# Moving work across the edges of the stages: weight gradients that start inside the GLU stage, an FFT chain paced ahead of them, and constants that are made first

## The chip, the cores and the metric

The kernel runs on one core of a Trainium2 chip. The metric is the device time of one execution in microseconds (us). The kernel before takes 695.69 us, the median of three runs (695.45 to 695.86). Engines are called PE (TensorE, the matrix engine), DVE (VectorE), ACT (ScalarE), POOL (GpSimd) and SP (SyncE, here a queue of DMA issues). Every engine works through its own instructions in program order.

## The reference

The kernel computes the output and all nine gradients of a gated block over 2048 tokens of width 512, in bfloat16. The forward function is:

```python
xn = layernorm(x)
# A: short convolution over 4 tokens, product with v, long convolution by FFT
k_shift = sum(k_pad[:, t:t + S] * shift_k[:, ks - 1 - t] for t in range(4))
kv = k_shift * v
y = irfft(rfft(kv_pad) * rfft(ssm_k_pad))[:S] + kv * ssm_D
s = xn * y
# B: gated linear unit, F = 1376
h = sigmoid(xn @ w_gate) * (xn @ w_up)
g = silu(h @ w_down)
out = x + s * g
```

`reference` returns `out` (out_0) and the gradients of `grad_out` with respect to q (out_1), k (out_2), v (out_3), shift_k (out_4), ssm_k (out_5), ssm_D (out_6), w_gate, w_up and w_down (out_7 to out_9).

## The kernel before

Tokens are cut into 16 tiles of 128, channels into four groups (cg) of 128, and F into 11 blocks of 128. The program has three stages.

**Stage A** (0 to 173 us) runs four generators side by side. `strK` and `strV` make the FFT's inputs from ssm_k and from the short convolution (`acc`, `term`, `kvt` on DVE), `strX` multiplies in the frequency domain and transforms back (tiles ps_q, ps_fl, ps_x, ps_b, ps_y), and `strG` runs the GLU's forward part (`f_gen`, tile psGU) for the first LAG = 3 token tiles. `gen_fft_consts` makes the FFT's matrices Cf, BD and R. The buffer `Bg` holds the last inverse step's input; ps_y reads it.

**The GLU stage** (173 to some 440 us) is `stepB`. For tile i it takes, in turn, `d_gen` (ps_dzT, psD), `f_gen` of tile i + 3 (ps_xnT, psGU), `z_gen` of tile i + 1 (psZ) and `x_gen` (psX). `z_gen` reads w_down in `wd`; `d_gen` reads its transpose `wdT`. Three arrays of results, h, dg and du, are turned by DMA transposes and stored to hS_d, dgS_d and duS_d in DRAM.

**The FFT backward stage** (to 660 us, and a drain) is `frontC` (ps_q) and `backC` (flips ps_fl, then ps_x, a complex product on DVE, ps_b, ps_y, ps_dk and ps_diag) for the four channel groups. Beside it `dW` makes the three weight gradients: 9 jobs, three sources times three column chunks (512, 512, 352), 35 blocks of 16 matmuls in all, tile psW. `ld_L(n)` loads the source of job n in four pieces, into one of two buffers in `Lbufs`.

Three things set the order. `run_streams` takes a list of generators with a budget, a start and an end: the one whose (start + (end − start) x work done / budget) is lowest goes next, so the numbers pace one generator against another. Tile's scheduler then reorders instructions within their dependencies. And `Bal.evac` gives each eviction from PSUM to ACT or DVE, whichever has the smaller sum of estimated work, unless the call names an engine. SBUF is one slab; a `Ring` is a piece of it, and freed pieces are handed out again, so a load into a new Ring waits for the last reader of the bytes that it covers.

PSUM: in stage A three two-bank tiles and two for transposes; in the later stages two two-bank tiles ("mm"), two for accumulation ("acc": psZ, psX, psW) and two for transposes.

Lines that the text speaks of (of the kernel before): L322 psGU, L325 the product that frees it, L596 the load of `wd`, L615 psZ, L626 the last product of dz, L660 psD, L679 psX, L749 `ld_L`, L765 and L768 psW, L121 and L124 the eviction on ACT and on DVE.

Of the kernel before, what the change touches and what calls it, by code (L numbers as in the profile page):

```python
# [16 lines left out]
P = 128  # L17
# [135 lines left out]
def gen_fft_consts(nc, ar, negpi, Cf, BD, R):  # L153
# [12 lines left out]
    m = tmp([16, 128], i32)  # L166
    mc = tmp([2, 16, 128], i32)
    for h in range(2):
        js = slice(8 * h, 8 * h + 8)
        nc.vector.tensor_tensor(m[:, js], a[:, js, None].to_broadcast([P, 8, 128]),  # L170
                                b[:, None, :].to_broadcast([P, 8, 128]), ALU.mult)
        nc.vector.tensor_single_scalar(mc[:, 0, js], m[:, js], 6144, ALU.add)
        nc.vector.tensor_single_scalar(mc[:, 0, js], mc[:, 0, js], 8191, ALU.bitwise_and)
        nc.vector.tensor_single_scalar(mc[:, 1, js], m[:, js], 8191, ALU.bitwise_and)
        nc.scalar.activation(Cf[:, :, js], mc[:, :, js], ACT.Sin, bias=negpi, scale=sc)
# [29 lines left out]
    for c, ci, t in ((0, 0, 0), (0, 1, 1), (1, 0, 2), (1, 1, 0)):  # L205
        nc.vector.tensor_scalar(R[:, c, :, :, ci], tri[:, t], SCALE_INV, None, ALU.mult)
    for r in rings:
        r.free()
# [7 lines left out]
def kernel_impl(ctx, tc, A_q, A_k, A_v, A_shift_k, A_ssm_k, A_ssm_D, B_x, B_w_gate, B_w_up, B_w_down,  # L216
# [19 lines left out]
    def ps_mm(shape, dt=f32, name="ps_mm"):  # L236
        return PS["pool"].tile([P] + shape, dt, name=name, tag="mm", bufs=PS["mm"])

    def ps_acc(shape, dt=f32, name="ps_acc"):
        return PS["pool"].tile([P] + shape, dt, name=name, tag="acc", bufs=2)  # L240

    def ps_tr(shape, dt=bf16, name="ps_tr"):
        return PS["pool"].tile([P] + shape, dt, name=name, tag="tr", bufs=2)
# [62 lines left out]
    def f_gen(i):  # L306
# [4 lines left out]
        bal.evac(xnT, pt[:], 512, half=True, eng="v")  # L311
# [5 lines left out]
        for pi, (f0, nb) in enumerate(FBS):  # L317
            ps = ps_mm([2, 4, 128], name="psGU")
            for k, w in ((0, wg), (1, wu)):
                for b in range(nb):  # L320
                    for db in range(4):
                        nc.tensor.matmul(ps[:, k, b, :], w[:, db, (f0 + b) * 128:(f0 + b + 1) * 128], xnT[:, db, :],  # L322
                                         start=(db == 0), stop=(db == 3))
            nc.scalar.activation(sigT[:, f0:f0 + nb, :], ps[:, 0, 0:nb, :], ACT.Sigmoid)  # L324
            nc.vector.tensor_tensor(hT[:, f0:f0 + nb, :], ps[:, 1, 0:nb, :], sigT[:, f0:f0 + nb, :], ALU.mult)  # L325
# [7 lines left out]

    psA = tc.tile_pool(name="psA", bufs=1, space=PSUM)
# [662 lines left out]
```

## Time and profile before

| what | value |
|---|---|
| median of 3 runs | 695.69 us |
| the profiled execution: its time, its span | 698.14 us, 696.4 us |
| PE busy | 558.4 us, 80% of the span |
| DVE busy | 440.2 us, 63% |
| ACT busy | 321.9 us, 46% |
| POOL busy | 143.3 us, 21% |
| moved by DMA | 114.51 MB, 164 GB/s on average |
| mean granted clock of PE | 0.94 |

In the rows that follow, a timeline row reads: start in us, length in us, engine, line, operation, tile written <- tile read, count of instructions, and in brackets the idle time ahead of it with what ended that. The matmuls of one row run one behind the other; the length covers the whole row. A row of windows reads: stretch, its length, busy time and number of instructions of PE, PE's weight loads, DVE, ACT and POOL, then the granted clock as a share, the busy share of DMA, and GB/s. A row of waits reads: who waited for whom, total us, number of times, longest.

### The profile page before, as it was taken

To read this page: it belongs to the slowest core of one execution; us is meant where nothing else is said; L and a number is where in the kernel's file an instruction comes from. 1 tells how busy PE (TensorE), PEld (TensorE's weight loads), DVE (VectorE), ACT (ScalarE), POOL (GpSimd) and SP (SyncE) were. 2 spreads that over 40 slices of the span, in tenths; PEclk is the share of its full clock that TensorE was granted. 3 is DMA by queue.
4 is the path that set the end of the run, shared out by engine and by line. 5 is a ranking of instruction groups with operands and counts; after the bars stand their busy time and mean duration, and the time that the engine had idled before them with its cause. 6 is when DMAs were issued, how large, how long until landed. Compare 5 with 4: busy or idle time off the path is not lost. (4 is left out here: it accounts for less than half of the span.)

```text
span 696.4 us, 12768 instructions
## 1 busy us (share of the span) xinstructions
PE 558.4 (80%) x5184; PEld 377.2 (54%) x5252; DVE 440.2 (63%) x888; ACT 321.9 (46%) x375; POOL 143.3 (21%) x242
## 2 busy tenths in 40 slices
PE   1577875976899999998999788469879999999800
PEld 0465754654666667766776445225455565656500
DVE  5988995645766777776776733203837739459450
ACT  4555693974333343342333213212582774664710
POOL 3022140331011111211111111131221243132020
PEclk9889998998999999999999999879999999999955
DMA  9444246497566666766767878955525479633094
GB/s 285 138 133 166 101 153 121 136 273 184 128 165 178 165 162 189 164 156 173 175 158 184 221 199 191 224 133 182 195 84 163 138 240 341 205 100 109 12 110 41
DMA packets 140962, 114.51 MB, mean 164 GB/s; under 512 B 91190, under 2 KB 126472, under 8 KB 140904
## 3 DMA queue, kind: packets, MB, share of 16 engines
q1 hardware_dynamic: 123224, 52.90, 34.2%
q0 software_dynamic: 16624, 57.98, 27.3%
q10 hardware_dynamic: 1056, 2.82, 1.1%
q8 instruction: 41, 0.67, 0.4%
q14 instruction: 17, 0.14, 0.1%
HBM read 49.18 MB, written 42.51 MB: 132 GB/s over the span
## 5 line engine op out<-in xcount | busy, mean ns | idle before, releaser
L322 PE MATMUL psGU<-slab 128*128 128x128 bf16 x1408 | 90.1, 223 | 9.0 <-DVE slab L325 4.7
L322 PEld LDWEIGHTS <-slab 128*128 128x128 bf16 x1408 | 85.1, 100 | 15.7 <-issue 13.7
L768 PE MATMUL psW<-slab 128*128 128x512 bf16 (+1 forms) x371 | 84.6, 356 | 1.1 <-ACT slab L121 0.5
L679 PE MATMUL psX<-slab 128*128 128x512 bf16 x336 | 79.6, 385 | 6.1 <-DVE slab L666 5.4
L121 ACT CAST slab<-ps_b 128x1024 bf16<-128x1024 f32 x48 | 49.0, 1023 | 37.8 <-PE ps_b L459 37.6
L459 PE MATMUL ps_b<-slab 128*128 128x256 bf16 x384 | 56.1, 279 | 12.0 <-DVE slab L448 10.6
L324 ACT ACTIVATE slab<-psGU 128x512 bf16<-128x512 f32 (+1 forms) x48 | 27.1, 564 | 69.3 <-PE psGU L322 69.2
L121 ACT CAST slab<-ps_x 128x1024 bf16<-128x1024 f32 x48 | 48.4, 1031 | 22.3 <-PE ps_x L439 21.5
L124 DVE COPY slab<-ps_fl 128x1024 bf16<-128x1024 bf16 x48 | 32.1, 687 | 40.3 <-PE ps_fl L428 40.0
L688 ACT ACTIVATE slab<-slab 128x512 f32<-128x512 f32 x16 | 13.1, 816 | 95.4 <-DVE slab L687 95.4
L679 PEld LDWEIGHTS <-slab 128*128 128x128 bf16 x352 | 33.3, 99 | 42.0 <-DVE slab L666 6.8
L121 ACT CAST slab<-ps_q 128x1024 bf16<-128x1024 f32 x48 | 48.6, 1044 | 15.4 <-PE ps_q L418 15.4
L765 PE MATMUL psW<-slab 128*128 128x512 bf16 (+1 forms) x172 | 40.9, 391 | 17.8 <-DMA slab<-hS_d 14.7
L459 PEld LDWEIGHTS <-slab 128*128 128x128 bf16 x384 | 35.5, 99 | 34.4 <-DVE slab L448 21.5
L768 PEld LDWEIGHTS <-slab 128*128 128x128 bf16 x384 | 36.6, 98 | 28.5 <-issue 0.8
L121 ACT CAST slab<-psW 128x512 bf16<-128x512 f32 (+2 forms) x35 | 20.3, 579 | 60.5 <-PE psW L765 40.9
L660 PE MATMUL psD<-slab 128*128 128x128 bf16 x704 | 46.3, 219 | 0.6 <-ACT slab L121 0.6
L660 PEld LDWEIGHTS <-slab 128*128 128x128 bf16 x704 | 41.8, 98 | 4.5 <-issue 0.7
L445 DVE TENSOR_TENSOR slab<-slab 128x1024 bf16<-128x1024 bf16 x48 | 33.1, 690 | 14.5 <-ACT slab L121 9.4
L615 PE MATMUL psZ<-slab 128*128 128x512 bf16 x162 | 39.7, 379 | 1.8 <-ACT slab L121 1.1
L418 PE MATMUL ps_q<-slab 128*128 128x128 bf16 x384 | 31.1, 230 | 11.4 <-DVE slab L518 5.3
L765 PEld LDWEIGHTS <-slab 128*128 128x128 bf16 (+1 forms) x176 | 17.9, 103 | 39.2 <-DMA slab<-hS_d 15.4
(154 smaller groups left out, 1008.1 us busy)
## 6 DMA issues: line engine op xcount, KB each, us to landing
KK_d<-slab POOLq DMA_DIRECT2D x32, 256.0 KB, 2.8
slab<-KK_d POOLq DMA_DIRECT2D x16, 512.0 KB, 4.2
out_dram<-slab POOLq DMA_DIRECT2D x58, 128.0 KB, 3.0
hS_d<-slab POOLq DMA_DIRECT2D x16, 352.0 KB, 2.7
dgS_d<-slab POOLq DMA_DIRECT2D x16, 352.0 KB, 3.8
duS_d<-slab POOLq DMA_DIRECT2D x16, 352.0 KB, 3.1
slab<-in_A_q_dram SPq DMA_DIRECT2D x32, 128.0 KB, 2.3
slab<-hS_d SPq DMA_DIRECT2D x8, 512.0 KB, 6.0
```

The costliest lines, as they stand in the source:

```text
L121: self.nc.scalar.copy(dst, src)
L124: self.nc.vector.tensor_copy(dst, src)
L322: nc.tensor.matmul(ps[:, k, b, :], w[:, db, (f0 + b) * 128:(f0 + b + 1) * 128], xnT[:, db, :], start=(db == 0), stop=(db == 3))
L324: nc.scalar.activation(sigT[:, f0:f0 + nb, :], ps[:, 0, 0:nb, :], ACT.Sigmoid)
L418: nc.tensor.matmul(ps[:, jj, :], Cf[:, c, j, :], src(j), start=True, stop=True)
L445: nc.vector.tensor_tensor(out=T1, in0=K, in1=X[:, 0:1, :].to_broadcast([P, 2, 512]), op=ALU.mult)
L459: nc.tensor.matmul(ps[:, gg].rearrange("p j x -> p (j x)"), Y[:, c, gg * 128:(gg + 1) * 128], R[:, c].rearrange("p j e c -> p (j e c)"), s ...
L615: nc.tensor.matmul(psZ[:], hT[:, fb, :], wd[:, fb, :], start=(fb == 0), stop=(fb == NFB - 1))
L660: nc.tensor.matmul(psD[:, b, :], wdT[:, db, (f0 + b) * 128:(f0 + b + 1) * 128], dzT[:, db, :], start=(db == 0), stop=(db == 3))
L679: nc.tensor.matmul(psX[:], srcT[:, fb, :], wT[:, fb, :], start=(n == 0), stop=(n == 2 * NFB - 1))
L765: nc.tensor.matmul(acc[0:kf, :], L[:, j, b * 128:b * 128 + kf], dzA[:, j, :], start=(j == 0), stop=(j == NJ - 1))
L768: nc.tensor.matmul(acc[:, 0:w], xnA[:, j, b * 128:(b + 1) * 128], L[:, j, 0:w], start=(j == 0), stop=(j == NJ - 1))
```

## The change

The change has five parts.

1. *Start.* `gen_fft_consts` is emitted first, and in it Cf behind BD and R. w_gate and w_up are loaded from SP's queue, behind the first q tile, ssm_k and k, where ACT issued them before; the second q tile and v come behind them. The loads of ssm_D and shift_k go from POOL's queue to ACT's.
2. *Evictions.* Those that named an engine (ps_xnT, ps_ci, ps_fl, ps_kt on DVE; ps_dzT on ACT) are now given by the balance.
3. *PSUM of the GLU stage.* In place of two two-bank tiles there are four of one bank: psG and psU apart, psD in blocks of 4, 4 and 3.
4. *Weight gradients.* The budget of `stepB` is set to the sum of its work (522 000 where it was 286 720), so dW's start at 0.9 lies beside its last tenth. `wd` and the five buffers of `z_gen` are freed when psZ of tile 15 is emitted; the second load buffer goes there, and loads 0 and 1 are both issued. The pieces of slab are laid out anew for that.
5. *FFT stage.* `frontC` is paced to 0.5 (before 0.75), `backC` from −0.05 to 0.72 (before 0.03 to 0.95), beside dW from 0 to 1.

```diff
@@ gen_fft_consts: the Cf part (m, mc, ACT.Sin) moves behind BD and R
...
@@ f_gen
-            ps = ps_mm([2, 4, 128], name="psGU")
-            for k, w in ((0, wg), (1, wu)):
+            if PS["wide"]:
+                ps = ps_mm([2, 4, 128], name="psGU")
+                pg, pu = ps[:, 0], ps[:, 1]
+            else:
+                pg, pu = ps_mm([4, 128], name="psG")[:], ps_mm([4, 128], name="psU")[:]
+            for pt_, w in ((pg, wg), (pu, wu)):
...
@@ stage A, start
     f_x(0)
-    nc.scalar.dma_start(wg[:, :, 0:F], B_w_gate.rearrange("(db p) f -> p db f", p=P))
-    nc.scalar.dma_start(wu[:, :, 0:F], B_w_up.rearrange("(db p) f -> p db f", p=P))
+    ld_KT(0)
+    ld_k(0)
+    nc.sync.dma_start(wg[:, :, 0:F], B_w_gate.rearrange("(db p) f -> p db f", p=P))
+    nc.sync.dma_start(wu[:, :, 0:F], B_w_up.rearrange("(db p) f -> p db f", p=P))
     f_x(1)
-    ld_KT(0)
-    ld_kv(0)
+    ld_v(0)
+    gen_fft_consts(nc, ar, negpi, Cf, BD, R)
...
@@ flip (and likewise ps_xnT, ps_ci, ps_kt; ps_dzT had eng="a")
-                bal.evac(Qf[:, c, gb * 8:(gb + 1) * 8, :], pt[:], 1024, half=True, eng="v")
+                bal.evac(Qf[:, c, gb * 8:(gb + 1) * 8, :], pt[:], 1024, half=True)
...
@@ GLU stage
-    psB = ctx.enter_context(tc.tile_pool(name="psB", bufs=1, space=PSUM, reuse_waits="tile"))
-    PS["pool"], PS["mm"] = psB, 2
+    PS["acc"] = ctx.enter_context(tc.tile_pool(name="psW", bufs=1, space=PSUM, reuse_waits="tile"))
+    psB = tc.tile_pool(name="psB", bufs=1, space=PSUM, reuse_waits="tile")
+    PS["mm"], PS["n"], PS["wide"] = psB.__enter__(), 4, False
...
+    zd_blk = ar.alloc(16384)
+    ar.release(zd_blk)
+    zw = {k: Ring(ar, [D]) for k in ("sigz", "gate", "s_out", "dgate", "t2")}
     wd_r, wdT_r, wgT_r, wuT_r = Ring(ar, [NFB, D]), Ring(ar, [4, FP]), Ring(ar, [NFB, D]), Ring(ar, [NFB, D])
...
@@ d_gen
-        for f0, nb in ((0, 8), (8, 3)):
-            psD = ps_mm([8, 128], name="psD")
+        for f0, nb in FBS:
+            psD = ps_mm([4, 128], name="psD")
...
@@ dW
                     stC["done", n] = True
-                    if len(Lbufs) > 1:
-                        ld_L(n + 2)
+                    ld_L(n + 2)
...
@@ the streams
-    live = run_streams([(gated(stepB(), "B"), 16 * 17920, 0.0, 1.0)], until=lambda: "fwd" in flags)
+    live = run_streams([(gated(stepB(), "B"), 522000, 0.0, 1.0)], until=lambda: "fwd" in flags)
     for r in (wg_r, wu_r, xq_r, xnT_r):
         r.free()
     Lbufs.append(Ring(ar, [NJ, 512]))
+    ot_r = Ring(ar, [512], n=3)
     live = run_streams(live, until=lambda: "z15" in flags)
-    ot_r = Ring(ar, [512], n=3)
-    ld_L(0)
-    live = run_streams(live + [(dW(), 35 * 8192, 0.9, 1.8)], until=lambda: "B" in flags)
-    for r in [wd_r, wdT_r, wgT_r, wuT_r, sig_r, h_r, xq2_r, go_r, dg_r, du_r, wq_r, dh_r,
-              dxa_r, dzT_r, dxn_r, u1_r, stS_r[0]] + list(zw.values()):
+    for r in [wd_r] + list(zw.values()):
         r.free()
     Lbufs.append(Ring(ar, [NJ, 512]))
+    ld_L(0)
+    ld_L(1)
+    live = run_streams(live + [(dW(), 35 * 8192, 0.9, 1.8)], until=lambda: "B" in flags)
...
-    ld_L(1)
-    if ("done", 0) in stC:
-        ld_L(2)
     dw = live[0]
-    p0 = dw[4] / dw[1]
-    run_streams([(dw[0], dw[1] - dw[4], 0.0, 1.0), (frontC(), 4 * 4096, 0.0, 0.75), (backC(), 4 * 43008 + 4096, 0.03, 0.95)])
+    run_streams([(dw[0], dw[1] - dw[4], 0.0, 1.0), (frontC(), 4 * 4096, 0.0, 0.5), (backC(), 4 * 43008 + 4096, -0.05, 0.72)])
```

How this moves instructions is shown at three places. The first is SP's queue where the GLU stage ends. hS_d<- rows are loads of h (L749 before, L762 after), 512 columns wide for jobs 0 and 1 and 352 for job 2; the transposes (L285) turn h, dg and du of the last tiles. Brackets name what a row waits for: an engine, or the DMA queues of SP (DMAHW) and POOL (DMASW). Before, from the last piece of load 0 on:

```order
L285 DMA_TRANSPOSE slab_65<-slab_65 128x11x128 [waits DMAHW3_49,DMASW0_49,DVE_49]
L749 DMA slab_65<-hS_d_59 128x4x352 [waits PE_49]
...
L749 DMA slab_65<-hS_d_59 128x4x352 [waits DMAHW7_49,PE_49]
L749 DMA slab_65<-hS_d_59 128x4x512 [waits DMAHW0_49,DVE_49,Activation_49]
L285 DMA_TRANSPOSE slab_65<-slab_65 128x11x128 [waits DMAHW1_49,DMASW1_49,DVE_49]
L285 DMA_TRANSPOSE slab_65<-slab_65 128x11x128 [waits DMAHW2_49,DMASW5_49,DVE_49]
L749 DMA slab_65<-hS_d_59 128x4x512 [waits DMAHW3_49,DVE_49,Activation_49]
L285 DMA_TRANSPOSE slab_65<-slab_65 128x11x128 [waits DMAHW4_49,DMASW6_49,DVE_49]
L285 DMA_TRANSPOSE slab_65<-slab_65 128x11x128 [waits DMAHW1_49,DMAHW5_49,DMASW6_49,DVE_49]
L749 DMA slab_65<-hS_d_59 128x4x512 [waits DMAHW6_49,Activation_49]
L749 DMA slab_65<-dgS_d_60 128x4x512 [waits DMAHW7_49,DMAHW3_49,PE_49]
```

And now:

```order
L762 DMA slab_65<-hS_d_59 128x4x512 [waits PE_49]
L762 DMA slab_65<-hS_d_59 128x4x512 [waits PE_49,Pool_49]
L762 DMA slab_65<-hS_d_59 128x4x512 [waits DMAHW7_49,DVE_49]
L762 DMA slab_65<-hS_d_59 128x4x512 [waits DMAHW0_49,DVE_49,Activation_49]
L285 DMA_TRANSPOSE slab_65<-slab_65 128x11x128 [waits DMAHW1_49,DMASW0_49,DVE_49]
L285 DMA_TRANSPOSE slab_65<-slab_65 128x11x128 [waits DMAHW2_49,DMAHW3_49,DMASW3_49,DVE_49]
L762 DMA slab_65<-hS_d_59 128x4x352 [waits PE_49]
...
L762 DMA slab_65<-hS_d_59 128x4x352 [waits DMAHW6_49,PE_49]
L285 DMA_TRANSPOSE slab_65<-slab_65 128x11x128 [waits DMAHW7_49,DMASW4_49,DVE_49]
L285 DMA_TRANSPOSE slab_65<-slab_65 128x11x128 [waits DMAHW0_49,DMAHW1_49,DMASW1_49,DVE_49]
L762 DMA slab_65<-dgS_d_60 128x4x512 [waits PE_49]
```

The four pieces of load 1 stand together, ahead of four transposes; before, the last three of them stood between and behind them.

The second place is SP's queue where stage A ends, with the load of `wd` (128x10x512). Before:

```order
L602 DMA_TRANSPOSE slab_65<-in_B_w_up_dram 128x10x512 [waits DMAHW3_49,PE_49]
L596 DMA slab_65<-in_B_w_down_dram 128x10x512 [waits DMAHW4_49,DVE_49,PE_49]
L597 DMA slab_65<-in_B_w_down_dram 96x512 [waits PE_49]
L600 DMA_TRANSPOSE slab_65<-in_B_w_down_dram 128x4x1376 [waits PE_49,Activation_49,Pool_49]
L604 DMA_TRANSPOSE slab_65<-slab_65 128x1x128
```

And now:

```order
L285 DMA_TRANSPOSE slab_65<-slab_65 128x11x128 [waits DMAHW5_49,DVE_49,PE_49]
L607 DMA slab_65<-in_grad_out_dram 128x512 [waits DMAHW6_49,PE_49]
L606 DMA slab_65<-in_A_q_dram 128x512 [waits DMAHW7_49,PE_49]
L606 DMA slab_65<-in_A_q_dram 128x512 [waits DMAHW0_49,PE_49]
L611 DMA slab_65<-in_B_w_down_dram 128x10x512 [waits DMAHW1_49,PE_49,Activation_49]
L607 DMA slab_65<-in_grad_out_dram 128x512 [waits DMAHW2_49]
```

The load went from ahead of the transposes of w_down and of the first tiles to behind the first loads of the GLU stage, and now waits for ACT where it waited for DVE. In the new layout its space covers the last 1280 bytes per partition of `Bg`.

The third place is POOL's queue at the end of the program, with the stores of out_2 to out_6 and of the last weight gradient, out_8. Before:

```order
L777 DMA out_8_dram<-slab_65 128x352 x2
L846 DMA slab_65<-slab_65 112x384
L847 DMA slab_65<-slab_65 15x384
L859 DMA out_5_dram<-slab_65 128x2048
L861 DMA out_3_dram<-slab_65 2048x1x256
L895 DMA out_6_dram<-slab_65 128x4x1
L894 DMA out_4_dram<-slab_65 128x4x4
L890 DMA out_2_dram<-slab_65 2048x1x256
```

And now:

```order
L859 DMA slab_65<-slab_65 15x384
L873 DMA out_3_dram<-slab_65 2048x1x256
L790 DMA out_8_dram<-slab_65 128x512
L871 DMA out_5_dram<-slab_65 128x2048
L907 DMA out_6_dram<-slab_65 128x4x1
L790 DMA out_8_dram<-slab_65 128x512
L906 DMA out_4_dram<-slab_65 128x4x4
L790 DMA out_8_dram<-slab_65 128x512
L790 DMA out_8_dram<-slab_65 128x352
L902 DMA out_2_dram<-slab_65 2048x1x256
L790 DMA out_8_dram<-slab_65 128x352 x3
```

All of dW's stores stood ahead of the last halo copies; now seven stand behind them, three of these behind the last store of the FFT chain. On PE, 80 psW matmuls (16 of 512 columns, 64 of 352) now stand behind the last ps_diag, where there were none.

More of the change, by code (lines that the diff above doesn't have):

```diff
@@ L206, in gen_fft_consts @@
         nc.vector.tensor_scalar(R[:, c, :, :, ci], tri[:, t], SCALE_INV, None, ALU.mult)
+    m = tmp([16, 128], i32)
+    mc = tmp([2, 16, 128], i32)
+    for h in range(2):
+        js = slice(8 * h, 8 * h + 8)
+        nc.vector.tensor_tensor(m[:, js], a[:, js, None].to_broadcast([P, 8, 128]),
+                                b[:, None, :].to_broadcast([P, 8, 128]), ALU.mult)
+        nc.vector.tensor_single_scalar(mc[:, 0, js], m[:, js], 6144, ALU.add)
+        nc.vector.tensor_single_scalar(mc[:, 0, js], mc[:, 0, js], 8191, ALU.bitwise_and)
+        nc.vector.tensor_single_scalar(mc[:, 1, js], m[:, js], 8191, ALU.bitwise_and)
+        nc.scalar.activation(Cf[:, :, js], mc[:, :, js], ACT.Sin, bias=negpi, scale=sc)
     for r in rings:
```

70 lines of the change are left out of this document (34 added, 36 removed).

## The prediction

> **What bounds the kernel now.** I read the page's forty slices first, to see where TensorE (PE) is not full, then the list of who waited for whom on PE, then PE's timeline at the places that the change touches. Each slice is 17.4 us.
>
> ```profile
> PE   1577875976899999998999788469879999999800
> ```
>
> PE is full from slice 11 to slice 21, dips in slices 24 to 27, is full again, and is empty in the last two. Ahead of slice 10 another engine sets the pace. In stage A, where the FFT's forward chain runs, that is VectorE (DVE). It is busy in nearly all of each stretch while PE has room:
>
> ```profile
> 60.00:80.00 20.00, 17.09 (x198) 13.48 (x199) 19.16 (x33) 15.24 (x17) 4.74 (x8) 1.00 0.30 109
> 80.00:100.00 20.00, 17.36 (x197) 13.19 (x199) 18.11 (x38) 17.96 (x22) 7.74 (x11) 1.00 0.44 152
> ```
>
> The third number is DVE: 19.16 and 18.11 of 20 us. Then PE's waits (total, times, longest):
>
> ```profile
> PE psW L765 <- DMA slab<-hS_d: 14.7, 2, 12.5
> ...
> PE ps_dzT L645 <- DVE slab L626: 5.8, 14, 1.4
> ...
> PE psGU L322 <- DVE slab L325: 4.7, 13, 0.7
> ```
>
> The longest is a wait of the weight gradients (psW) for their second load of hS_d. It stands where the GLU stage ends and the FFT backward stage begins:
>
> ```profile
> 407.09 3.40 PE L765 MATMUL psW<-slab 128*128 128x512 bf16 x14 [0.70 <-DVE slab L685]
> ...
> 442.70 1.90 PE L765 MATMUL psW<-slab 128*128 128x512 bf16 x8 [2.18 <-DMA slab<-hS_d]
> 444.44 1.06 PE L418 MATMUL ps_q<-slab 128*128 128x128 bf16 x16
> 458.01 1.89 PE L765 MATMUL psW<-slab 128*128 128x512 bf16 x4 [12.52 <-DMA slab<-hS_d]
> 460.12 19.91 PE L765 MATMUL psW<-slab 128*128 128x512 bf16 x86 [0.22 <-issue]
> 479.86 1.06 PE L428 MATMUL ps_fl<-slab 128*128 128x128 bf16 x16
> ```
>
> The FFT chain's first flip (ps_fl) stands behind all of it, at 479.86. The queue of SyncE (SP) gives the cause: the last piece of that load is issued only at 443.35, because pieces of it stand behind transposes that need the last tile's results.
>
> ```profile
> 443.35 0.56 SPq L749 DMA_DIRECT2D slab<-hS_d  x1
> ```
>
> The FFT backward stage, cut at the last ps_diag matmul of each of the four channel groups (columns: length, PE, weight loads, DVE, ScalarE (ACT), POOL, clock, DMA):
>
> ```profile
> 479.90:519.60 39.70, 33.90 (x277) 21.27 (x281) 25.30 (x44) 25.44 (x20) 7.17 (x13) 0.96 0.38 122
> 519.60:571.60 52.00, 50.56 (x371) 29.82 (x376) 31.78 (x49) 33.00 (x31) 13.18 (x21) 1.00 0.58 182
> 571.60:621.20 49.60, 48.51 (x356) 29.80 (x361) 31.16 (x49) 30.56 (x28) 15.37 (x25) 1.00 0.69 221
> 621.20:660.20 39.00, 36.30 (x273) 23.72 (x275) 28.84 (x48) 21.53 (x22) 8.89 (x14) 0.96 0.25 79
> 660.20:696.40 36.20, 0.00 (x0) 0.00 (x0) 10.89 (x14) 4.08 (x1) 4.40 (x5) 0.54 0.69 73
> ```
>
> PE limits the two middle groups (50.56 of 52.00, 48.51 of 49.60). The last 36.2 us hold no PE work: DVE ends the shift gradient, and the last large store drains.
>
> ```profile
> 670.04 1.22 DVE L886 TENSOR_TENSOR slab<-slab 128x2048 bf16<-128x2048 bf16 x1
> 671.56 1.12 POOL L890 DMA_DIRECT2D out_dram<-slab  x1 [3.71 <-DVE slab L886]
> ```
>
> From that issue to the span's end are 24.8 us. Weight-gradient work that runs under this drain costs nothing, and before it none does.
>
> **The change, part by part.** The sum is made against the profiled execution's span of 696.4 us. Its own time is 698.14, and the median of the runs shown, 695.69, lies 0.7 below the span. I take that 0.7 off at the end.
>
> *The join.* From the first psW (407.09) to the first flip (479.86) are 72.8 us. The change frees w_down's space when tile 15's psZ is through and issues load 1 there, ahead of the last transposes. Load 1 then has job 0's 64 psW matmuls and what stands between them as cover, some 30 us by the old trace. Both waits go: 2.18 + 12.52 = 14.7. The price of one psW matmul follows from two neighbouring rows:
>
> ```profile
> 525.87 5.99 PE L768 MATMUL psW<-slab 128*128 128x512 bf16 x27
> 531.70 1.06 PE L428 MATMUL ps_fl<-slab 128*128 128x128 bf16 x16
> ```
>
> (531.70 − 525.87) / 27 = 0.216 us for 512 columns; for one of 352 columns I take its share by width, 0.149. In the new order 132 psW matmuls stand ahead of the first flip where 160 stood: 28 x 0.216 = 6.0 less. After the long wait 4 matmuls took 1.89 us and 86 took 19.91; at 0.216 they are 0.9 and 18.6, so the wait cost 2.3 more in slow matmuls. Together 23.0; with the small waits beside it I take 24.5. Bounds: 6.0, if the load still arrives late, to 28.
>
> *The FFT stage.* Its chain is paced ahead (budget to 0.72 where it was 0.95), so psW matmuls move out of the groups in which they filled PE. Their cost in each stretch, by count in the two orders: to the first flip 34.6 before and 28.5 after; then by group 6.0, 27.0, 27.5, 13.9 before and 7.3, 14.3, 23.4, 22.5 after; behind the last ps_diag 0 and 13.0. The rest of PE's work in a group is its busy time less the old psW: 27.9, 23.6, 21.0, 22.4. New PE work per group: 35.2, 37.9, 44.4, 44.9. To each comes idle time that psW cannot fill: the first group had 5.8, the full ones 1.4 and 1.1, the last, with the same small filler as the new second one, 2.7. With 5.8, 3.1, 1.1 and 1.1 I get 41.0, 41.0, 45.5, 46.0 = 173.5 where 180.3 stood: **−6.8**. All flips now go to ACT, four more evacuations a group at about the 1.0 us of this row, with ACT busy 25 of 40 us in the first group before and 33 of 52 in the second. Bounds: −16 (next to no idle) to +6 (rival 2).
>
> ```profile
> L121 ACT CAST slab<-ps_b 128x1024 bf16<-128x1024 f32 x48 | 49.0, 1023 | 37.8 <-PE ps_b L459 37.6
> ```
>
> *The tail.* The drain from the last ps_diag stays at 36.2, and 13.0 us of psW run below it. On POOL's queue the last results of that work stand around the store of L890, three of them behind it. I add 1, bounds 0 and 6.
>
> *w_down arrives late.* The change lays w_down's space over the last bytes of stage A's Bg buffer, which the last ps_y matmuls read; so its load moves from the middle of stage A to behind them.
>
> ```profile
> 142.37 0.52 SPq L596 DMA_DIRECT2D slab<-in_B_w_down_dram  x1
> ...
> 169.20 3.25 PE L471 MATMUL ps_y<-slab 128*128 128x128 bf16 x32 [1.10 <-ACT slab L121]
> 173.55 4.91 PE L615 MATMUL psZ<-slab 128*128 128x512 bf16 x21 [1.10 <-ACT slab L121]
> ```
> ```profile
> slab<-in_B_w_down_dram SPq DMA_DIRECT2D x1, 1280.0 KB, 7.3
> ```
>
> ps_y ends at 172.45. With 7.3 to land, the first psZ starts at 179.8 and not at 173.55: 6.2 late, and behind it stands everything on PE, which sets the pace of the GLU stage. PE would be idle for 7 us; the row at 458.01 shows what follows (4 matmuls in 1.89 us), so I take **+7**, bounds +3 (a quicker landing) to +9. The Trainium skill ("TensorE: Matmul & The Clock Gate", Part 1) says that an idle window of about 3.4 us halves the clock until the array has been busy as long again; the row at 458.01 agrees (0.47 a matmul). By it the loss behind the gap would be 1.7 us and the term 7.9.
>
> *GLU steady state.*
>
> ```profile
> 289.81 2.54 PE L615 MATMUL psZ<-slab 128*128 128x512 bf16 x10
> ...
> 305.77 1.46 PE L615 MATMUL psZ<-slab 128*128 128x512 bf16 x5
> ```
>
> One tile takes 15.96 us. Four one-bank PSUM tiles take the place of two of two banks. The 4.7 us of waits for DVE L325 have room to go, and psX is now ahead of ps_dzT, so the 5.8 for L626 too; but psD's second block must now wait for a bank that DVE frees after psU's first. A full win is −10.5; walking the new order gave half a microsecond per tile. I take **−4**, bounds −10.5 and +3.
>
> *The start.* Constants come first on DVE, ahead of the shift chain's first multiply, and the wg and wu loads move from ACT's queue to SP's, ahead of the second q tile and v.
>
> ```profile
> 19.09 1.22 DVE L508 TENSOR_TENSOR slab<-slab 128x2048 bf16<-128x2048 bf16 x1
> ```
> ```profile
> GB/s 285 138 133 166 101 153 121 136 273 184 128 165 178 165 162 189 164 156 173 175 158 184 221 199 191 224 133 182 195 84 163 138 240 341 205 100 109 12 110 41
> ```
>
> Stage A is bound by DVE, and its work there is the same to within 3 us (nine more evacuations on ACT, other ones back). In the new order the shift chain stands behind the layer norm of the third q tile, whose load is the last of 5.9 MB on SP's queue: at the 285 GB/s of the first slice they take 21 us, so with the issue it lands two to five us after 19.09. While it waits the constants are made, which are needed anyway. I take 0, bounds −4 and +5. The Trainium skill ("DMA: Bandwidth & Descriptors", section on issuing engines) says that all transfers share the same 16 engines whoever issues them. By it the move of the two loads gains nothing but issue time, and the term stays 0. The loads of D and shift_k, moved to ACT's queue, and the new pool of PSUM at the FFT stage I cost at nothing: DVE's constants and the psW matmuls hide them; bare, an eviction or two, 1 to 2 us, which the bounds hold.
>
> Sum: 696.4 − 24.5 − 6.8 + 1 + 7 − 4 + 0 = 669.1; less 0.7, **668.4 us**, 3.9% faster.
>
> **The rivals.** 1. *Forecast*, chance 0.55.
>
> 2. *The chain becomes the bound of the FFT stage.* With less filler each group is held by the relay ps_x, ACT, cmul on DVE, ps_b, ACT. For it: ACT takes all the flips and evacuates ps_dk in one long row,
>
> ```profile
> 560.96 8.87 ACT L121 CAST slab<-ps_dk 128x1024 bf16<-128x1024 f32 x2 [0.25 <-PE ps_dk L856]
> ```
>
> behind which the next group's evacuations queue. Against it: the last group before took 39.0 with 13.9 of filler. At 46 to 47 a group, 186 instead of 173.5: about 681. Chance 0.2.
>
> 3. *The load is late all the same*, because pieces of load 1 wait on SP for DVE and ACT. The join's 14.7 and 2.3 come back: about 685. For it: the second pair of load 1 waits for engines that also serve tile 15. Against it: that work is done some 10 us before job 1. Chance 0.08.
>
> 4. *The GLU stage loses its stalls altogether* (−10.5, 6.5 more than taken) and w_down lands sooner (3 less): about 659. Chance 0.08.
>
> 5. *Slower.* The chain paced ahead is held by ACT in every group: evacuations, all flips and the 8.87 of ps_dk in a row, each waited for by PE. First flip now at 458.4 (479.86 − 24.5 + 7 − 4), drain 37.2; so 696.4 is reached when the four groups take 200.8, or 50.2 each. From 9 us idle per group on average, three times the 2.8 of before, this decides; at 52 each the time is 703. Against it: ACT was busy no more than 33.0 in any group. Chance 0.05.
>
> 6. *The change does little at the join*: the pieces of dW emitted beside tiles 14 and 15 delay the last GLU tiles as much as they fill. Then the 24.5 there are lost again: about 693. Chance 0.04.
>
> **How the numbers follow.** A measurement of this kernel tells about 0.2% (1.4 us) from no change. Cases 1 to 4 and 6 are faster but for a sliver: faster 0.92, same 0.03, slower 0.05. The range takes in rivals 2 and 4 and the bounds of the start and of w_down: 653 to 685; rivals 5 and 6 and half of 3 lie outside.
>
> **What would show it.** Join: no wait of psW for hS_d over 1 us, first flip 47 to 50 us after the first psW. Tail: psW matmuls for 13 us behind the last ps_diag, 36 to 38 us from it to the end. Groups: 41, 41, 45 to 46, 46. w_down: a gap of 5 to 7 us ahead of the first psZ, with DMA as its releaser. GLU: 15.5 to 15.8 per tile. Start: the first psZ, less that gap, at 170 to 178. The prediction is wrong if a group takes over 48, if psW waits for a load again, or if stage A moves by more than 6.

## The result, and the profile after

The changed kernel takes 658.65 us (median of 4 runs), 0.950 of the kernel before (95% interval 0.945 to 0.956), 5.0% less. The ratio compares means, and one of the four runs of the kernel before took 688.90; by the medians it is 0.947. Where the runs of a kernel spread by more than 1.5%, the ratio leaves some of them out and the median does not, so the two can differ by a per cent. The forecast was 668.4, in a range of 653 to 685. The profiled execution has a span of 659.8 us and a time of 661.59, 2.9 above the median.

PE in forty slices (16.5 us each now), and PE's waits as in the prediction:

```profile
PE   0576898787389998999999988999979979999992
```
```profile
PE ps_xnT L309 <- ACT slab L301: 17.3, 1, 17.3
PE psZ L630 <- DMA slab<-in_B_w_down_dram: 9.7, 1, 9.7
...
PE psW L781 <- ACT slab L121: 7.7, 1, 7.7
...
PE ps_dzT L660 <- DVE slab L641: 1.4, 2, 1.0
```

The dip in the middle and the two empty slices at the end are gone. So are the wait of psW for hS_d and that of psG and psU for DVE, and ps_dzT's fell from 5.8 to 1.4. The first slice is now empty. The large new waits are three: PE's first transpose of xn for the layer norm on ACT (ps_xnT, at the start of the program), the first psZ for w_down, and a late psW for ACT. The join in PE's timeline:

```profile
411.45 0.38 PE L778 MATMUL psW<-slab 128*128 128x512 bf16 x1 [2.28 <-DVE slab L698]
...
452.92 4.48 PE L778 MATMUL psW<-slab 128*128 128x512 bf16 x20
457.23 1.06 PE L438 MATMUL ps_fl<-slab 128*128 128x128 bf16 x16
```

From the first psW to the first flip are 45.8 us; it was 72.8. The FFT stage, cut at the last ps_diag of each group (columns as in the prediction):

```profile
457.23:498.90 41.67, 36.23 (x281) 21.68 (x285) 20.09 (x36) 32.13 (x28) 7.23 (x12) 0.96 0.48 154
498.90:545.20 46.30, 41.59 (x310) 24.30 (x314) 29.05 (x45) 34.86 (x31) 12.07 (x18) 0.93 0.54 164
545.20:589.90 44.70, 44.36 (x349) 29.12 (x352) 29.02 (x45) 33.98 (x32) 12.96 (x21) 1.00 0.74 230
589.90:632.97 43.07, 42.10 (x292) 24.58 (x296) 29.01 (x45) 29.83 (x27) 10.41 (x16) 1.00 0.46 143
632.97:659.80 26.83, 14.57 (x80) 8.12 (x78) 8.83 (x12) 2.68 (x6) 6.97 (x11) 0.83 0.62 88
```

The whole is best read as stretches of PE's timeline, cut at rows that both kernels have. All are in us, each from the profile of one execution: end of the last ps_y of stage A; from there to the first psZ; from the first psZ to the first ps_dzT; to the first psW; to the first flip; to the end of the last ps_diag; to the end of the span. A small negative number means that the two rows overlap.

| kernel | stage A | to psZ | psZ | GLU | join | FFT | drain | span |
|---|---|---|---|---|---|---|---|---|
| before | 172.4 | 1.1 | 5.8 | 227.7 | 72.8 | 180.3 | 36.2 | 696.4 |
| changed | 172.3 | 9.7 | 8.1 | 221.4 | 45.8 | 175.7 | 26.8 | 659.8 |
| changed, once more | 172.7 | 9.7 | 8.2 | 219.5 | 45.4 | 172.9 | 28.4 | 656.8 |
| w_down clear of Bg | 177.3 | −0.2 | 6.0 | 220.1 | 45.3 | 175.5 | 29.6 | 653.5 |
| small outputs as rows | 168.2 | 10.7 | 7.6 | 218.9 | 45.4 | 172.7 | 19.3 | 642.8 |
| old paces | 171.4 | 9.8 | 8.2 | 222.8 | 53.9 | 179.2 | 37.6 | 682.8 |
| load 1 late | 169.4 | 8.5 | 8.2 | 221.8 | 49.8 | 178.1 | 30.9 | 666.8 |
| old start | 168.9 | 10.5 | 7.2 | 217.9 | 45.4 | 175.4 | 29.0 | 654.3 |
| old evictions | 171.4 | 12.3 | 8.2 | 218.5 | 45.7 | 176.4 | 30.9 | 663.4 |
| wide PSUM tiles | 172.4 | −0.2 | 6.3 | 226.8 | 48.4 | 174.3 | 30.0 | 657.9 |
| before, new paces | 173.2 | 1.1 | 5.8 | 226.5 | 64.5 | 177.2 | 28.4 | 676.8 |
| before, rows | 170.9 | 1.1 | 5.8 | 226.9 | 66.9 | 179.0 | 19.9 | 670.6 |
| rows, clear, old start | 172.1 | −0.2 | 6.1 | 219.5 | 45.8 | 175.5 | 19.2 | 637.9 |

Stage A ends between 168.2 and 172.7 in the changed kernel's two profiles and in those with rows, old paces and load 1 late, whose edits do not touch it; so a difference of 3 or 4 us in that column is no effect of an edit by itself. "Ratio" below is to the kernel before on the same chip.

### The profile page after: what moved, and what is told of

The parts are those of the page before. It is cut to its first block, busy times and chain, and to the rows that moved or that the text cites. A ratio compares the mean times of both kernels' runs of the same rounds, so it can differ in the third digit from the quotient of the medians.

```text
span 659.8 us, 12885 instructions
## 1 busy us (share of the span) xinstructions
PE 560.9 (85%) x5198; PEld 376.1 (57%) x5252; DVE 428.0 (65%) x875; ACT 355.2 (54%) x433; POOL 142.3 (22%) x240
## 5 line engine op out<-in xcount | busy, mean ns | idle before, releaser
L781 PE MATMUL psW<-slab 128*128 128x512 bf16 (+1 forms) x372 | 86.4, 364 | 8.3 <-ACT slab L121 7.7
L692 PEld LDWEIGHTS <-slab 128*128 128x128 bf16 x352 | 33.4, 99 | 49.0 <-DVE slab L679 12.3
L121 ACT COPY slab<-ps_dzT 128x512 bf16<-128x512 bf16 x16 | 9.3, 584 | 85.3 <-PE ps_dzT L660 85.3
L630 PE MATMUL psZ<-slab 128*128 128x512 bf16 x175 | 42.8, 393 | 9.9 <-DMA slab<-in_B_w_down_dram 9.7
L121 ACT CAST slab<-ps_x 128x1024 bf16<-128x1024 f32 x43 | 43.6, 1027 | 14.1 <-PE ps_x L449 13.1
L121 ACT CAST slab<-ps_q 128x1024 bf16<-128x1024 f32 x45 | 45.6, 1045 | 6.6 <-PE ps_q L428 6.6
L778 PE MATMUL psW<-slab 128*128 128x512 bf16 (+1 forms) x171 | 44.1, 390 | 2.7 <-DVE slab L698 2.3
L678 ACT CAST slab<-psD 128x512 bf16<-128x512 f32 (+1 forms) x48 | 26.1, 544 | 33.0 <-PE psD L675 32.6
L326 PE MATMUL psU<-slab 128*128 128x128 bf16 x572 | 38.3, 219 | 0.0
L326 PE MATMUL psG<-slab 128*128 128x128 bf16 x572 | 38.3, 219 | 0.0
L281 POOL DMA_DIRECT2D dgS_d<-slab x16 | 8.7, 543 | 134.9 <-DMA slab<-slab 134.9
```

Of the source, the lines that this page charges most:

```text
L121: self.nc.scalar.copy(dst, src)
L326: nc.tensor.matmul(pt_[:, b, :], w[:, db, (f0 + b) * 128:(f0 + b + 1) * 128], xnT[:, db, :], start=(db == 0), stop=(db == 3))
L630: nc.tensor.matmul(psZ[:], hT[:, fb, :], wd[:, fb, :], start=(fb == 0), stop=(fb == NFB - 1))
L678: nc.scalar.copy(dh[:, 0:nb, :], psD[:, 0:nb, :])
L692: nc.tensor.matmul(psX[:], srcT[:, fb, :], wT[:, fb, :], start=(n == 0), stop=(n == 2 * NFB - 1))
L778: nc.tensor.matmul(acc[0:kf, :], L[:, j, b * 128:b * 128 + kf], dzA[:, j, :], start=(j == 0), stop=(j == NJ - 1))
```

## The experiments

Runs whose edit is to "the changed kernel" have all its other parts. The changed kernel, run once more beside later runs, is the measure for them:

> The changed kernel itself, unaltered, as the measure for the other runs on the same chip. Every theory expects the ratio of the first measurement, 0.950 to the kernel before, within its interval (0.945 to 0.956), about 658; its profile shows how far stage A's end and the drain move from one execution to the next.

Measured: 659.03 (656.85 to 665.49), ratio 0.951 (0.947 to 0.955). The result stands.

**w_down clear of Bg.** Edit:

```diff
+    dg_r = Ring(ar, [NFB, 128], n=2)
     zd_blk = ar.alloc(16384)
...
-    dg_r, du_r = Ring(ar, [NFB, 128], n=2), Ring(ar, [NFB, 128], n=2)
+    du_r = Ring(ar, [NFB, 128], n=2)
```

> The changed kernel with the ring of dg laid ahead of the block of w_down, so that w_down's space lies clear of Bg and its load is issued in stage A again. Theory: the changed kernel's 9.7 us wait of the first psZ for w_down and the slow psZ behind it (6.31 us for 20 matmuls) are lost time, since PE sets the pace of the GLU stage; both go, 10 to 11 us less than the changed kernel (658.65), about 648. Rival: stage A leaves work on DVE and ACT that the gap covers, and the GLU stage's first tiles wait for it instead; 0 to 4 us less.

Measured: a median of 657.12, over six runs in two groups: 649.15, 653.00 and 655.24 (the profiled one), and 659.01, 659.42 and 659.91. The recorded ratio, 0.952 (0.949 to 0.955), is that of the upper three. The middle of the lower three is some 6 us under the changed kernel, the upper three are level with it. So the gain lies between nothing and some 6 us, less than the theory's 10 to 11 and nearer to the rival. The profile shows why it can be less. The gap is gone, but the last ps_y comes 5 us later, with a longer wait of PE for DVE in stage A:

```profile
173.70 3.57 PE L481 MATMUL ps_y<-slab 128*128 128x128 bf16 x32 [1.10 <-ACT slab L121]
177.07 5.00 PE L631 MATMUL psZ<-slab 128*128 128x512 bf16 x21
```
```profile
PE ps_x L446 <- DVE slab L124: 8.2, 1, 8.2
```

That wait was 5.8 in the changed kernel and 6.2 once more. On SP's queue four transposes of w_gate's last block now stand ahead of four loads of q, where two stood, and DVE's layer norm waits for these loads up to 9.6 us, where it waited 7.2 and 7.7. But this is not shown to be what delays stage A. The kernel with wide PSUM tiles, further down, also loads w_down in stage A and has nearly the same waits, 9.0 us of DVE and this one of PE, and its stage A ends at 172.4:

```profile
PE ps_x L446 <- DVE slab L124: 7.6, 1, 7.6
```

In the last run of this study four transposes stand ahead of the q loads too, and stage A ends at 172.1. So with its load back in stage A the kernel may lose there what it wins at the gap, and need not; what decides it stays open.

**Small outputs as rows.** Edit, at the end of `backC`:

```diff
-        with nc.allow_non_contiguous_dma(reason="small output"):
-            nc.gpsimd.dma_start(out_4.rearrange("(db p) t -> p db t", p=P), skout)
-            nc.gpsimd.dma_start(out_6.rearrange("(cg p) -> p cg", p=P), dDo)
+        pt = ps_tr([5, 128], name="ps_small")
+        for lag in range(4):
+            nc.tensor.transpose(pt[0:NG, lag, :], skout[:, :, lag], ident)
+        nc.tensor.transpose(pt[0:NG, 4, :], dDo, ident)
+        nc.vector.tensor_copy(sm4.rearrange("p d t -> p t d"), pt[0:NG, 0:4, :])
+        nc.vector.tensor_copy(sm6, pt[0:NG, 4, :])
+        nc.gpsimd.dma_start(out_4.rearrange("(db p) t -> db p t", p=P), sm4)
+        nc.gpsimd.dma_start(out_6.rearrange("(cg p) -> cg p", p=P), sm6)
...
+    sm4_r, sm6_r = Ring(ar, [128, 4]), Ring(ar, [128])
+    sm4, sm6 = sm4_r.ap[0:NG], sm6_r.ap[0:NG]
```

> The changed kernel with out_4 and out_6 turned on PE first and stored as 4 rows of 1024 and 256 bytes, in place of elements of 8 and 2 bytes. Theory: in the changed kernel the small stores hold up the store of out_8 behind them, whose buffer the next psW eviction needs (ACT waits 11.4 us for it, PE 7.68): that wait goes, and the end comes 6 to 8 us earlier, about 651. Rival: the 512-byte rows of out_2 and out_3 and the 1 MB under way are what is slow; then less than 2 us.

Measured: 646.99, ratio 0.936 (0.930 to 0.941), 10 to 12 under the changed kernel. What the changed kernel's tail showed, in the order ACT, POOL, PE:

```profile
650.82 0.87 ACT L121 CAST slab<-psW 128x352 bf16<-128x352 f32 x2 [11.42 <-DMA out_dram<-slab]
```
```profile
634.19 0.77 POOL L907 DMA_DIRECT2D out_dram<-slab  x1
634.95 0.54 POOL L790 DMA_DIRECT2D out_dram<-slab  x1
637.40 0.76 POOL L906 DMA_DIRECT2D out_dram<-slab  x1 [1.91 <-DVE slab L904]
```
```profile
651.32 3.90 PE L781 MATMUL psW<-slab 128*128 128x352 bf16 x16 [7.68 <-ACT slab L121]
```

The stores of out_6 (L907) and out_4 (L906) are issued at 634.19 and 637.40. A store of dW's (L790) between them takes 15.8 us to land, so that the eviction which needs its buffer starts only at 650.82, and the last 16 matmuls wait for that. Landing times of that store, of out_6 and of out_4 in the changed kernel, then of out_4 and out_6 as rows:

```profile
out_dram<-slab POOLq DMA_DIRECT2D x1, 128.0 KB, 15.8
out_dram<-slab POOLq DMA_DIRECT2D x1, 1.0 KB, 16.3
out_dram<-slab POOLq DMA_DIRECT2D x1, 4.0 KB, 13.5
```
```profile
out_dram<-slab POOLq DMA_DIRECT2D x1, 4.0 KB, 1.6
out_dram<-slab POOLq DMA_DIRECT2D x1, 1.0 KB, 1.5
```

The drain falls from 26.8 to 19.3 and the wait of psW is gone. These 7.5 us are within the theory's 6 to 8; the rest of the difference lies outside the tail (stage A 4 us shorter in this profile) and is not explained.

**The same in the kernel before.**

> The kernel before with nothing changed but out_4 and out_6 turned on PE and stored as rows. Theory: the drain of 36.2 us from the last ps_diag is long because the element-wise stores of out_4 and out_6 fill the DMA engines (2.15 and 0.93 busy at 74 and 18 GB/s behind the issue of out_2); as rows out_2 lands in about 8 us and not in 24, so 13 to 17 us less than before: 678 to 682. Rival: the two 1 MB stores and out_2's 512-byte rows need that time; under 4 us.

Measured: a median of 681.28 over four runs from 672.47 (the profiled one) to 683.58, 13 us under the 694.12 of the kernel before beside it; the ratio, 0.974 (0.967 to 0.981), makes it 18. The drain is 19.9 where it was 36.2. In the kernel before, this is what moved behind the issue of out_2 (DMA share and GB/s are the last two numbers; the share counts a packet's whole time where it starts, so that it can pass 1):

```profile
672.00:676.00 4.00, 0.00 (x0) 0.00 (x0) 0.00 (x0) 0.00 (x0) 0.68 (x1) 0.50 2.15 74
676.00:680.00 4.00, 0.00 (x0) 0.00 (x0) 0.00 (x0) 0.00 (x0) 0.00 (x0) 0.50 0.93 18
```

The packets under way take long and move little. The landing times of out_2, out_6 and out_4 before, and then of out_2 with rows:

```profile
out_dram<-slab POOLq DMA_DIRECT2D x1, 1024.0 KB, 23.0
out_dram<-slab POOLq DMA_DIRECT2D x1, 1.0 KB, 24.8
out_dram<-slab POOLq DMA_DIRECT2D x1, 4.0 KB, 24.2
```
```profile
out_dram<-slab POOLq DMA_DIRECT2D x1, 1024.0 KB, 6.0
```

So 16 of the 36 us of drain that the prediction took as given were, by the profiles, the price of 5 KB in elements; by the runs it is 13 to 18.

**The paces.** Edit:

```diff
-    run_streams([..., (frontC(), 4 * 4096, 0.0, 0.5), (backC(), 4 * 43008 + 4096, -0.05, 0.72)])
+    run_streams([..., (frontC(), 4 * 4096, 0.0, 0.75), (backC(), 4 * 43008 + 4096, 0.03, 0.95)])
```

> The changed kernel with the old paces of the last stage (frontC to 0.75, backC 0.03 to 0.95). The order has 34.6 us of psW ahead of the first flip again and none behind the last ps_diag. Theory (the prediction's terms): 13 us of psW move out from under the drain onto the path, the drain goes back to some 36 us, the groups get back 1 to 3 us of idle time: 8 to 16 us slower than the changed kernel, 667 to 675. Rival: the pace only shifts filler between groups; within 3 us of 658.65.

Measured: 677.97, ratio 0.980 (0.974 to 0.986): 19 slower, more than the theory's 8 to 16. By stretches of its profile, which is of the longest of its four runs (684.66): join +8.1, FFT +3.5, drain +10.8. The drain is 37.6 again, so the rest of the change does not shorten it without the new paces. The same edit the other way round, alone in the kernel before:

> The kernel before with nothing changed but the paces of the last stage (frontC to 0.5, backC from -0.05 to 0.72). 28 psW matmuls go from ahead of the first flip, 13.0 us of them stand behind the last ps_diag. Theory: the pace is worth here what it is worth in the changed kernel (677.97 without it against 658.65), 13 to 20 us, and the join's wait of 14.7 for hS_d stays: 675 to 681. Rival: the pace pays only where load 1 is early, as the chain waits behind that load all the same; under 8 us.

Measured: 678.87, ratio 0.980 (0.977 to 0.982), 14.5 less. The drain is 28.4 there too, so the paces do it alone. psW still waits at the join:

```profile
PE psW L765 <- DMA slab<-hS_d: 12.1, 2, 10.7
```

**Load 1 late.** w_down's space is held to the end of the GLU stage, so that the second buffer is found there as before; no other part is undone.

```diff
+    ld_L(0)
+    live = run_streams(live + [(dW(), 35 * 8192, 0.9, 1.8)], until=lambda: "B" in flags)
     for r in [wd_r] + list(zw.values()):
         r.free()
-    Lbufs.append(Ring(ar, [NJ, 512]))
-    ld_L(0)
-    ld_L(1)
-    live = run_streams(live + [(dW(), 35 * 8192, 0.9, 1.8)], until=lambda: "B" in flags)
...
     PS["n"] = 2
+    Lbufs.append(Ring(ar, [NJ, 512]))
...
     ld_KK(1)
+    ld_L(1)
```

> The changed kernel with w_down's space held to the end of the GLU stage, so load 1 gets its old kind of buffer and its pieces stand between the last transposes again; budget, paces and all else stay new, and PE's order too. Theory: the wait of psW for hS_d comes back at the join, 12 to 17 us slower than the changed kernel, 670 to 676. Rival: with dW's pieces spread between the last tiles load 1 is needed later than before, so that most of the wait is hidden: 0 to 5 us slower.

Measured: 667.06, ratio 0.964 (0.959 to 0.970): 8 slower, between the two. PE's wait for the load is 3.4 us, not 14.7:

```profile
PE psW L781 <- ACT slab L121: 11.1, 1, 11.1
...
PE psW L778 <- DMA slab<-hS_d: 3.4, 1, 3.4
```

The join is 4.0 longer; the FFT stage and the drain hold the rest (the wait for ACT is the one of the tail). So most of the old wait stays hidden even where the load is late. The 28 matmuls moved out are not what hides it, since 12.1 us of it stayed with them in the kernel before. That leaves dW's new order, spread between the last tiles, as the likely reason; no run has that order alone.

**The start.** The loads of ssm_D and shift_k also go back to POOL's queue; inside the constants Cf stays behind BD and R.

```diff
     f_x(0)
-    ld_KT(0)
-    ld_k(0)
-    nc.sync.dma_start(wg[:, :, 0:F], ...)
-    nc.sync.dma_start(wu[:, :, 0:F], ...)
+    nc.scalar.dma_start(wg[:, :, 0:F], ...)
+    nc.scalar.dma_start(wu[:, :, 0:F], ...)
     f_x(1)
+    ld_KT(0)
+    ld_k(0)
     ld_v(0)
-    gen_fft_consts(nc, ar, negpi, Cf, BD, R)
...
     f_ln(0)
+    gen_fft_consts(nc, ar, negpi, Cf, BD, R)
```

> The changed kernel with the start undone: constants emitted behind the first layer norm, w_gate and w_up issued from ACT's queue at once, ssm_D and shift_k from POOL's. Theory (the prediction's term of 0): the shift chain starts 5 us earlier (19 and not 24), but the last product of it comes at 102 us either way, so the end of stage A and the time stay within 3 us of the changed kernel. Rival: the new start is part of the gain, 5 us or more slower without it.

Measured: 657.77, ratio 0.947 (0.943 to 0.951), 1.3 under the changed kernel beside it: as the theory had it, no effect that can be told.

**The evictions.** `eng="v"` for ps_xnT, ps_ci, ps_fl and ps_kt, `eng="a"` for ps_dzT, as in:

```diff
-                bal.evac(Qf[:, c, gb * 8:(gb + 1) * 8, :], pt[:], 1024, half=True)
+                bal.evac(Qf[:, c, gb * 8:(gb + 1) * 8, :], pt[:], 1024, half=True, eng="v")
```

> The changed kernel with the evictions of ps_xnT, ps_ci, ps_fl and ps_kt on DVE and of ps_dzT on ACT again, as before. Theory (the prediction's term of 0): who evicts these tiles moves stage A's DVE work by under 3 us and the FFT stage's chain by as much the other way; within 3 us of the changed kernel, ratio 0.946 to 0.956 to the kernel before. Rival: with the flips on ACT the changed kernel pays 8.1 us (ps_q) and 3.7 us (ps_fl) of PE's waits for ACT, which DVE would spare: 5 us or more faster.

Measured: 667.16, ratio 0.961 (0.958 to 0.964): 8 slower on medians, 7 by the ratios. Both views are wrong: the balance is worth something. PE's three longest waits but one (that of ps_xnT at the start, 17.1, which the runs with the new start have):

```profile
PE psZ L630 <- DMA slab<-in_B_w_down_dram: 12.3, 1, 12.3
PE psW L781 <- ACT slab L121: 10.5, 1, 10.5
PE ps_fl L438 <- DVE slab L124: 10.0, 8, 3.0
```

The flips wait 10.0 for DVE, where they waited 3.7 for ACT and 1.5 for DVE; the FFT stage is 0.7 to 3.5 longer than in the two profiles of the changed kernel, the gap ahead of psZ 2.6 and the drain 2.5 to 4.1. Why the last two should follow from the evictions was not tested.

**Wide PSUM tiles.** psG and psU share a tile again:

```diff
-    PS["mm"], PS["n"], PS["wide"] = psB.__enter__(), 4, False
+    PS["mm"], PS["n"], PS["wide"] = psB.__enter__(), 2, True
...
-        for f0, nb in FBS:
-            psD = ps_mm([4, 128], name="psD")
+        for f0, nb in ((0, 8), (8, 3)):
+            psD = ps_mm([8, 128], name="psD")
```

The wider dh ring that this needs moves w_down's space by 2048 bytes, clear of Bg, so the gap ahead of psZ goes as well: the run holds two edits, and only the GLU column tells of PSUM.

> The changed kernel with the old PSUM of the GLU stage: two tiles of two banks, psD in blocks of 8 and 3, psG and psU in one tile. Theory: the 6 to 8 us that the GLU stage got shorter (227.7 before, 219.5 to 221.4 in the changed kernel from the first ps_dzT to the first psW) come from the four one-bank tiles: 5 to 8 us slower than the changed kernel, the waits of psGU for DVE back near 4.7 us. Rival: they come from the new order of psX, ps_dzT and ps_xnT that the changed budget and evictions gave; within 2 us.

Measured: 662.38, ratio 0.955 (0.952 to 0.958). The GLU stage takes 226.8, as before, 5.4 to 7.3 more than in the changed kernel's two profiles, and the waits of psGU for DVE are back:

```profile
PE psGU L326 <- DVE slab L329: 4.5, 13, 0.6
```

One tile, psZ to psZ, in the changed kernel and then in this one:

```profile
282.04 2.54 PE L630 MATMUL psZ<-slab 128*128 128x512 bf16 x11
...
297.38 2.54 PE L630 MATMUL psZ<-slab 128*128 128x512 bf16 x11
```
```profile
272.80 2.54 PE L630 MATMUL psZ<-slab 128*128 128x512 bf16 x11
...
288.75 2.54 PE L630 MATMUL psZ<-slab 128*128 128x512 bf16 x11
```

15.34 against 15.95 (15.96 before): 0.6 us a tile are the one-bank tiles' work.

**The best parts together.** First rows and clear space in one kernel:

> Both mends in the changed kernel: small outputs as rows, and w_down clear of Bg. Theory: the drain is free of the small stores, and the gap ahead of the first psZ goes; where w_down clear of Bg was worth 6 us of span in its profile alone, less a stage A that ended 5 us later: 16 us under the changed kernel, 639 to 645, that is 3 to 6 us under the run with rows alone (646.99). Rival: w_down's load in stage A costs what the gap costs, since it runs beside the transposes and loads on which stage A waits; equal to rows alone, 645 to 649.

Measured: 646.53, ratio 0.929 (0.925 to 0.934). That is 0.6% under rows alone, less than the intervals can settle, and at the rival's end; its profile is of the longest of its six runs (652.64), so it is not in the table. Then with half the shift (one of dg's two buffers laid ahead of the block) and the old start:

```diff
+    dg_r = Ring(ar, [NFB, 128])
     zd_blk = ar.alloc(16384)
...
-    dg_r, du_r = Ring(ar, [NFB, 128], n=2), Ring(ar, [NFB, 128], n=2)
+    dg2_r, du_r = Ring(ar, [NFB, 128]), Ring(ar, [NFB, 128], n=2)
+    dg_r.blks += dg2_r.blks
+    dg_r.aps += dg2_r.aps
```

> The best parts together: the changed kernel with small outputs as rows, with w_down clear of Bg by one ring of dg (2816 bytes, half the shift of the run before), and with the old start. Theory: the rows are worth 11, the gap ahead of the first psZ goes but stage A ends later because its loads of q stand behind more transposes on SP; 0.925 to 0.932 to the kernel before, 640 to 647. Rival: the smaller shift leaves SP's order in stage A as it is in the changed kernel and the whole gap is won: 0.918 or less, 637 or less.

Measured: 639.64, ratio 0.921 (0.919 to 0.924). It is the fastest kernel of this study, 7.9% under the one before, between what theory and rival had. Here the gap is gone and stage A ends where it did:

```profile
168.49 3.57 PE L483 MATMUL ps_y<-slab 128*128 128x128 bf16 x32 [1.10 <-ACT slab L121]
171.86 5.09 PE L635 MATMUL psZ<-slab 128*128 128x512 bf16 x22
```

Whether the smaller shift or the old start keeps stage A short here was not separated.

## Why the prediction was right, point by point

Against the span of 696.4 the terms were −24.5, −6.8, +1, +7, −4 and 0, together −27.3. Measured, span against span: −36.6.

- *Join, −24.5 forecast:* −27.0, within the bounds (28). Both waits for load 1 are gone, and the slow matmuls behind them. From 411.98 to the first flip PE has no wait over 0.2 us; the small waits of the old join (2.05, 0.94, 1.01 and 0.40) come to 4.4, and the term had 1.5 for them. The number was right, but the cause is only in part the one named. The prediction put all 14.7 us down to the early load; with the load late only 3.4 of them come back and the join is 4 us longer. With the old paces it is 8 longer.
- *FFT stage and drain, −6.8 and +1:* −4.6 and −9.4. The drain is the step that failed: it was taken as a fixed 36.2, with 1 added, and was 26.8, in spite of the new wait of 7.68 in it. The prediction read the 24.8 us behind the last issue as the landing of a large store; the two runs with rows show that the small stores of out_4 and out_6 made most of it. Under the new paces the 1 MB store of out_3 is issued 16.5 us ahead of out_2 (625.84 and 642.30), where 6.4 us lay between them (665.15 and 671.56). It lands in 6.0 us, before the small stores are issued; in the kernel before it ran beside them and took 22.3. Part of the 9.4 is only the mark, because psW matmuls now stand among the last ps_diag. The end of the last ps_dk, which comes just ahead of them, tells how much. Before, then now:

```profile
654.26 2.06 PE L856 MATMUL ps_dk<-slab 128*128 128x128 bf16 x32
```
```profile
624.14 1.06 PE L868 MATMUL ps_dk<-slab 128*128 128x128 bf16 x16
```

  From there to the span's end are 40.0 us before and 34.6 now (36.2 once more). So some 4 of the 9.4 went from the drain to the FFT column, and 4 to 5 are a shorter drain. Counted to that row, the FFT stage took 168.0 where it took 176.5.

  The groups were forecast at 41.0, 41.0, 45.5, 46.0 and took 41.7, 46.3, 44.7, 43.1: the sum is 2 off. The second had 41.6 of PE work and 4.7 idle, where 37.9 and 3.1 were forecast. Most of its idle time is one wait for ACT, which was in its row of ps_dk; this is the wait that rival 2 names. The first group had it before and has it still, the second has it new, and the last two have none:

```profile
531.09 8.90 ACT L121 CAST slab<-ps_dk 128x1024 bf16<-128x1024 f32 x2
```
```profile
535.64 0.27 PE L428 MATMUL ps_q<-slab 128*128 128x128 bf16 x1 [3.35 <-ACT slab L121]
```

  The granted clock was 0.93 in that group. In the changed kernel's second profile the same wait is there, the clock is 1.00, and the group takes 43.5:

```profile
496.78:540.29 43.51, 38.81 (x309) 23.34 (x313) 29.04 (x45) 34.85 (x31) 12.12 (x18) 1.00 0.53 158
```

- *w_down, +7:* +10.9 (8.6 in the gap, 2.3 in psZ), past the upper bound of 9. Mechanism and place were right; the load took 9.3 to land and not 7.3, and the 20 matmuls behind the gap took 6.31, 0.32 each, where 21 had taken 4.91:

```profile
172.64 0.39 SPq L611 DMA_DIRECT2D slab<-in_B_w_down_dram  x1
```
```profile
168.69 3.57 PE L481 MATMUL ps_y<-slab 128*128 128x128 bf16 x32 [1.10 <-ACT slab L121]
181.96 0.61 PE L630 MATMUL psZ<-slab 128*128 128x512 bf16 x1 [9.70 <-DMA slab<-in_B_w_down_dram]
182.79 6.31 PE L630 MATMUL psZ<-slab 128*128 128x512 bf16 x20 [0.22 <-issue]
```
```profile
slab<-in_B_w_down_dram SPq DMA_DIRECT2D x1, 1280.0 KB, 9.3
```

  The slow matmuls that the prediction took from the row at 458.01 show here too, with the granted clock at 0.50 (third number from the end):

```profile
181.96:186.00 4.04, 3.82 (x9) 1.45 (x11) 0.00 (x0) 0.00 (x0) 0.54 (x1) 0.50 0.44 108
```

  They cost 2.3 us behind 9.7 idle. The Trainium skill ("TensorE: Matmul & The Clock Gate", Part 1) puts a halved clock behind an idle window; by its figure the loss was estimated at 1.7. That the price comes back where the gap is taken away is a second question: with w_down clear of Bg it came back in part or not at all, while the profiles with wide PSUM tiles and of the last run have no gap and a stage A no longer than the changed kernel's.
- *GLU, −4:* −6.3 (−8.2 once more). The cause (one-bank tiles) was right, shown by the run with wide ones: 15.34 a tile for 15.96, about the half microsecond that walking the order had given, which the term then took only in part.
- *Start, 0:* stage A ends at 172.3 for 172.4, and the run with the old start is within 0.4%. The shift chain did start late, and by 102 us had made it up: first multiply and last product in the changed kernel are

```profile
24.35 1.23 DVE L518 TENSOR_TENSOR slab<-slab 128x2048 bf16<-128x2048 bf16 x1
```
```profile
L528 DVE TENSOR_TENSOR slab<-slab x4: 1210/1214/1219, 35.5 to 101.9; 128x2048 bf16<-128x2048 bf16 x4
```

  and were 19.09 and 102.1. The evictions, costed at nothing with it, are worth 7 to 8 us, in places not settled.

Rivals 3, 5 and 6 did not occur. The time is nearly that of rival 4 (659), but not by its cause: the GLU stage won 6.3 of its 10.5, and w_down came later, not sooner. Too low a wait for w_down and too long a drain stood on opposite sides, and the drain was the larger: the forecast was 10 us too high, and that the errors offset each other in part was luck. Of the signs that the prediction gave, four missed: the first flip came 45.8 us after the first psW (47 to 50), the drain was 26.8 (36 to 38), the gap 9.7 (5 to 7) and a GLU tile 15.34 (15.5 to 15.8). None of the three that it would have taken as proof against it was seen. Its 0.2% for what a measurement can tell was too small; six runs of the changed kernel span 656.85 to 665.49.

## What to carry to other kernels

A drain at the end of a profile is a term like any other: ask which store lands last, and whether the DMA engines are busy while few bytes move. When a ring of buffers is laid anew, look up which last reader each first load then waits for; 1280 bytes of overlap cost 11 us at the first psZ here. Filler that can run under a drain is worth more there than in stages that are already full.

## What the runs showed of the hardware

Two stores of 5 KB in all, in pieces of 8 and 2 bytes, took 24 to 25 us to land in the kernel before, and the two 1 MB stores beside them 22.3 and 23.0. Turned on PE into rows of 1024 and 256 bytes, for five small matmuls and two copies, they landed in 2.7 and 1.7 us there, and out_2 beside them in 6.0. The DMA packets of the two traces show where the time went: the 640 packets of 4096 bytes that start behind the last ps_diag took 391 us together, the longest 13.7, and with rows 137 and 0.34. The 32 packets of the two small stores are recorded with 5 us in all. So the small stores slowed the packets of the large ones.

The Trainium skill ("DMA: Bandwidth & Descriptors", the rules for kernel authors) says that a last dimension that is not contiguous becomes one descriptor per element and should be rearranged. That is the form of out_6; out_4 went in runs of four elements. No trace here counts descriptors; the runs show the price of both stores together: 16 us of drain in the kernel before, 7.5 in the changed one.

Behind 9.7 us without a matmul the granted clock was 0.50 for the first 4 us, and 20 matmuls of 512 columns took 0.32 us each, where 21 at a granted clock of 1.00 took 0.23.
